# An attention and gated-MLP kernel: the order of its last six batches written out piece by piece

## The chip, the cores and the metric

The kernel runs on one core of one Trainium2 chip. The metric is the device time of one execution in microseconds (us). The core has TensorE for matrix products (PE in the rows, its weight loads PEld), VectorE (DVE), ScalarE (ACT), GpSimd (POOL) and SyncE (SP), which here only issues DMA transfers.

## The reference

Eight batches pass through three stages:

```python
# attention, 8 heads, 576 positions, 64 wide, 32 packed queries p
p_packed = sm_attn(p, k, v)               # softmax(p k^T / 8) v
out = sm_attn(q, p_packed, p_packed)      # softmax(q pp^T / 8) pp
x = out, heads side by side               # 576 x 512
# gated layer
gate = sigmoid(sum_k conv_w[k] * x shifted by 4 - k positions)
x = (gate * (x @ w_val)) @ w_out
# spatial MLP
h = relu(x @ w_in); u, v = halves of h    # 576 x 512 each
v_n = (v - mean(v)) / sqrt(var(v) + 1e-6)
v_s = w_spatial @ v_n + b_spatial         # mixes the 576 positions
return (u * v_s) @ w_out2
```

## The kernel before

All big products are made from pairs of a rounded value and its residue (`hi`, `lo`), three matmuls for each block of 128 rows: hi by hi, hi by lo, lo by hi (`mm3`, L120). The split into `hi` and `lo` is an ACT cast followed by a DVE subtraction (`split`, L114 and L116). The work of a batch is cut into pieces, each a Python generator; every `yield` ends one step of it. The pieces, in the order in which one batch needs them:

- `sa`: scores of the packed queries, 32 small matmuls into two PSUM tiles (64 records in the trace), then row maxima on DVE and the exponentials on ACT (L170 to L194). `tr`, `av`, `ppt`: transpose, product with v, transposed result `pp`.
- `sb`, `sn`, `sb2`: second attention, its softmax, and the matrices `A` in hi and lo.
- `m`: product of pp and w_val (`Mh`, `Ml`). `xt`: the attention's output x. `cv`: the convolution of x as four DVE operations in place on one tile `acc` (L350), then the gate (a sigmoid on ACT). There are four `cv`, one for each block of 128 channels.
- `val`: value products, 12 matmuls of 288 columns each, the product with the gate (L380), the split into g tiles, a copy of the tail.
- `hv`: 12 matmuls of 512 columns for each of four blocks of positions, 8 for the tail; normalization (statistics on DVE, a power on POOL, a DVE scaling, split) into `vn`. `hu`: 24 matmuls for each of four blocks, and a relu into `u`.
- `sp`: the spatial product, 28 matmuls for each of four blocks; then product with u (L480) and split into g tiles. `out`: the output product, 24 matmuls for each of four blocks; ACT copy, DMA out.

Pieces that belong to the attention of batch b+1 run beside the MLP of batch b, and next to the last pieces of batch b the `val` of batch b+1 begins. `lk`, `lq`, `lv`, `lp` issue loads on SP's queue for batches still further ahead. In the head there are also the conversion of the float64 weights (`uo`, `uw`, `uv`, `uu`: an ACT operation, three DVE operations, a POOL addition), products of two weight matrices (`fold`), and the setup of `ws` and `wo`.

Shared tiles set limits: four PSUM tiles serve all pieces, and four g tiles hold first the split values (`val`), then the split results of `sp`. A value of the next batch can therefore not be split before the last `out` matmul of this one has read its g tiles.

Two rules set the order. The string HEAD is taken literally, token by token (`tc.manual_schedule`): `0sp3.1` takes one step of piece sp3 of batch 0, `0sp3` the rest of it. The string LOOP is run for each batch from 2 to 7 outside of that, and there a scheduler reorders single instructions by a timeline of its own, so that matmuls of two pieces can alternate.

Of the kernel before, what the change touches and what calls it, by code (L numbers as in the profile page):

```python
# [20 lines left out]
HEAD = """
ro1.1 cb0.1 ip0 ro0 ic0 ik0 rw1 rw0.1 uo2.1 ik1 uo2.1 lk0 uo0.1 lp0 uo2 uo0.1 uo1.1 ro1 cw0.1 iv1 uo1.1 uo0 iv0 cw0.1
uw2.1 uo1 rv0.1 uw2.1 cw0 uw3.1 rv0 cb0.1 uw3.1 uw0.1 uw2 rw0 cb0.1 sa0.1 uw0.1 uw3 lq0 cb0.1 uw0 sa0.1 lq1 0ws2.1 cb0
uo3.1 0ws3.1 uo3.1 sa0.1 0ws0.1 sa0 tr0 uo3 0ru0.1 av0.1 tr1 uv0.1 0ru0 uv0.1 av1.1 uv1.1 lv0 av0.1 uv0 av1.1 av0.1
uw1.1 0ws4.1 av0 av1.1 ppt0.1 av1 uv1.1 lv1 ppt0 sb0 uw1.1 0lp0 uv1 0ru1.1 rv1.1 uw1 fv1.1 sn0.1 rv1 0uu0.1 fv1.1 lk1
sn1.1 sn0 0ws1.1 fv1.2 sb20.1 0wo0.1 sn1 fv0.1 fv1.1 0ru1 fv0.2 fv1 sb20.1 fv0.1 sb21.1 fv3.1 fv0.1 uv2.1 fv3.2 uv3.1
uv2.1 fv3.1 sb21.1 cx0.1 fv3.1 sb21 uv2 fv3 fv0 sb20 cx1.1 uv3.1 cx0 0uu0.1 uv3 m0.1 cx1 0uu0 fv2.1 0uu1.1 fv2.1 m0.1
0uu1.1 fv2.2 m0 0uu1 0val3.1 fv2 0uu2.1 0val3.1 0uu2.1 0val0.1 0val1.1 0val3.1 0uu2 0val2.1 0val3.1 0val0.1 0val3
0uu3.1 0val2.1 0val0.1 0val1.1 0val2.1 0val0.1 0sa0.1 0uu3.1 0val2.1 0lq0 0val1.1 0uu3 0fu0.1 1lp0 0sa0.1 0lq1 0val1.1
0fu0.1 0wo0.1 0fu0.2 0fu3.1 0fu0.1 0val1 0fu3.1 0sa0.1 0fu0 0fu3.1 0val0 0fu3.1 0val2 0hv0.1 0fu3.1 0tr0 0sa0 0fu3  # L30
0wo0.1 0hv1.1 0hv0.1 0tr1 0wo1.1 0wo0.1 0hv0.2 0fu2.1 0hv0.1 0hv1.1 0hv0.1 0fu2.1 0hv1.1 0wo1.1 0fu2.1 0wo1.1 0hv1.1
0fu2.1 0hv3.1 0hv1.1 0wo3.1 0fu2.1 0wo1.1 0hv0 0hv1.1 0wo1.1 0hv1 0fu2 0hv4.1 0hv3.1 0wo3.1 0hv3.1 0hv2.1 0wo3.1
0hv4.1 0hv3.1 0hv4.1 0lk0 0wo3.1 0hv3.1 0hv4.1 0av0.1 0wo3.1 0hv4.1 0av1.1 0hv3.1 0lv0 0fu1.1 0hv3 0lv1 0hv4.1 0av0.1
0hv2.1 0fu1.1 0hv4.1 0av0 0av1.1 0hv4.1 0fu1.1 0hv2.1 0av1 0ppt0.1 0fu1.1 0hv4 0ppt0 0hv2.2 0sb0 0ws3.1 0wo1 0fu1.1
0ws3 0m0.1 0ws4.2 0fu1 0lk1 0hv2.1 0wo2.1 0sn1.1 0hu0.1 0ws0.1 0ws2.1 0m0.1 0hu0.1 0ws4.1 0m0 0sn1 0ws4.1 0hu1.1 0hu0
0sb21.1 0ws4.1 0wo2.1 0hu1.1 0ws1.1 0wo0.1 0hu2.1 0hu1 0wo2.1 0sb21.1 0hu3.1 0ws2 1lq0 0wo2.1 0ws4 0hu3.1 0wo2.1 0ws1
0hu2.1 0sb21 0hu3 0wo3 0hv2 1sa0.1 0hu2 0ws0 0sn0.1 1lq1 0sp2.1 1lk1 0sp2.1 1sa0.1 0sn0 0sp0.1 1lk0 0sb20.1 1sa0.1
0sp0.1 1sa0 0sp3.1 0sp2.1 0sb20.1 0sp0.1 0sp2.1 0sb20 0sp1.1 0sp0.1 0sp2 0sp0 0sp1.1 1tr0 1tr1 0wo0 0xt0.1 0sp1.1
0sp3.1 0wo2 0sp1.1 0xt0 0sp1 0xt1.1 0sp3.1 1av0.1 0sp3.1 1av1.1 0xt1 1av0.1 1lv0 0sp3 0out2.1 1lv1 1av0 1av1.1 0cv1.1
0cv3.1 0cv1.1 0out2.1 1av1 0cv2.1 0cv0.1 0out3.1 0out2 0cv3.1 0cv1 0out0.2 0cv2.1 0cv3 0out1.1 0out0 0out1.1 0cv0.1  # L40
0cv2 1val1.1 0out1.1 1val1.1 0out1 0out3.1 1val1.1 0cv0 1val1.1 1val0.1 0out3.1 1val1 1val0.1 0out3 1val2.1 1val0.1
1val2.1 1val0.1 1ppt0.1 1val0 1val3.1 1ppt0 1val2.1 1val3.1 1val2.1 1sb0 1val3.1 1val2 1val3.1 1m0.1 1val3 1hv1.1
1sn0.1 1m0 1sn0 1hu1.1 1sn1.1 1hv0.1 1hv1.2 1sn1 1hv3.1 1sb21.1 1hv0.1 1hv1.2 1hv2.1 1sb21.1 1hv0.1 1hv1.1 1sb21
1hv0.1 1hv1 1hv0.1 1hu0.1 1hv3.1 1sb20.1 1hv0.1 1hu0.1 1hv0 1sb20.1 1hu1.1 1hv3.1 1hv2.1 1hu0 1hv2.1 1hv4.1 1hu1
1hv3.2 1hv2.1 1sb20 1hv3.1 1hu2.1 1hv3 1hv2.1 1hv4.1 1hv2.1 1hu3.1 1hv4.1 1hv2 1hv4.2 1hu3.1 1hv4.1 1hu2.1 1hu3 1hv4
1sp1.1 1hu2 1sp1.1 1sp2.1 1sp1 1sp2.1 1sp3.1 1sp2 1sp0.2 1xt0.1 1sp0.1 1sp3.1 1sp0.1 1xt0 1sp0 1xt1.1 1sp3.2 1xt1 1sp3
1out0.1 1cv1.1 1out0.1 1cv3.1 1cv1.1 1cv0.1 1out3.1 1out0.1 1cv2.1 1out0 1out3.1 1cv3.1 1cv1 1out2.1 1out3 1out1.1
1cv0.1 1cv3 1out1.1 1out2.1 1cv2.1 1cv0 1out1 1out2 1cv2
"""
# [712 lines left out]
```

## Time and profile before

| what | value |
|---|---|
| median of 3 runs (lowest, highest) | 615.42 us (615.08, 616.09) |
| profiled execution, its time | 615.56 us |
| span of that execution in the trace | 613.6 us |
| TensorE matmul busy | 581.7 us, 95% of the span |
| VectorE, ScalarE busy | 451.1 us (74%), 291.9 us (48%) |
| granted TensorE clock, all slices | full |

The time is taken outside of the trace and is about 2 us longer than the span. Busy time of TensorE is modelled from starts of matmuls, so a matmul that occupies it longer than it needs is counted as busy.

### The profile page before, as it was taken

What the parts mean: (1) busy time and instruction counts of PE and PEld (TensorE: products, weight loads), DVE (VectorE), ACT (ScalarE), POOL (GpSimd) and SP (SyncE); (2) the same over time, 40 slices, a digit from 0 to 9 for tenths busy, and PEclk for the clock granted to TensorE, in tenths of its full rate; (3) what the DMA queues carried; (4) which work ended last, traced back from release to release, by engine and by line L of the source; (5) the groups of instructions that cost most, each with busy time, mean ns of one, the idle gap of its engine ahead of it and who ended that gap; (6) DMA issues with size and microseconds to landing.
All of it is one profiled execution on the core that took longest, in us unless ns stands there. A gap on an engine that the chain in (4) does not pass through costs nothing.

```text
span 613.6 us, 12468 instructions
## 1 busy us (share of the span) xinstructions
PE 581.7 (95%) x5267; PEld 507.2 (83%) x5267; DVE 451.1 (74%) x868; ACT 291.9 (48%) x503; POOL 54.7 (9%) x72
## 2 busy tenths in 40 slices
...
GB/s 315 409 373 3 95 126 182 90 1 72 171 1 21 59 83 154 12 59 103 89 78 20 62 80 164 2 60 96 89 78 20 74 25 2 1 78 2 1 1 77
DMA packets 16615, 52.55 MB, mean 86 GB/s; under 512 B 1968, under 2 KB 2992, under 8 KB 16560
## 3 DMA queue, kind: packets, MB, share of 16 engines
...
q8 instruction: 41, 0.67, 0.4%
...
## 4 chain that ended last, share of the span: by engine, by line
PE 74%; DVE 7%; ACT 3%; issue 1%; ACTq 0%
PE ps L120 68%; DVE acc L350 2%; PE ps L170 2%; PE ps L311 1%; DVE mx L178 1%; PE ps L213 1%; ACT L194 1%; PE ps L248 1%; PE ps L295 1%; ACT a L194 1%; DVE g L116 1%; ACT g L114 1%; DVE nb L189 1%; DVE m L184 1%; DVE g L480 0%
## 5 line engine op out<-in xcount | busy, mean ns | idle before, releaser
L120 PE MATMUL ps<-ws,vn 128*128 128x288 f32 (+1 forms) x896 | 124.0, 296 | 0.0
L120 PEld LDWEIGHTS ps<-ws,vn 128*128 128x128 f32 (+1 forms) x896 | 120.2, 188 | 3.5 <-issue 3.4
L120 PE MATMUL ps<-g,wp 128*128 128x288 f32 x768 | 112.4, 297 | 0.8 <-DVE wp L568 0.8
L120 PEld LDWEIGHTS ps<-g,wp 128*128 128x128 f32 x768 | 106.5, 188 | 5.3 <-DVE wp L568 1.7
L120 PEld LDWEIGHTS ps<-g,wo 128*128 128x128 f32 x768 | 102.2, 188 | 5.5 <-issue 2.6
L120 PE MATMUL ps<-g,wo 128*128 128x288 f32 x768 | 105.5, 296 | 0.3 <-DVE g L116 0.2
L120 PE MATMUL ps<-wp,g 128*128 128x512 f32 x384 | 97.8, 402 | 3.1 <-ACT a L194 2.7
L350 DVE SCALAR_TENSOR_TENSOR acc<-x,cw,acc 128x572 f32<-128x572 f32 (+3 forms) x112 | 84.7, 815 | 20.5 <-ACT acc L346 19.7
L120 PEld LDWEIGHTS ps<-wp,g 128*128 128x128 f32 x384 | 70.0, 188 | 22.5 <-ACT a L194 4.5
L114 ACT CAST g<-g 128x576 fp32r<-128x576 f32 x64 | 43.2, 675 | 77.8 <-DVE g L480 59.5
L427 POOL TENSOR_TENSOR rstd<-rstd,mhalf 128x1 f32<-128x1 f32 (+1 forms) x40 | 23.4, 587 | 464.0 <-DVE rstd L425 464.0
L116 DVE TENSOR_TENSOR g<-g,g 128x576 fp32r<-128x576 f32 x64 | 48.3, 756 | 12.5 <-ACT g L114 11.9
L421 DVE BATCH_NORM_STATS2 st<-vr 128x6 f32<-128x512 f32 (+1 forms) x40 | 27.5, 689 | 26.3 <-ACT vr L409 23.7
L480 DVE TENSOR_TENSOR g<-ps,u 128x576 f32<-128x576 f32 x32 | 24.0, 754 | 23.3 <-PE ps L120 23.3
L114 ACT CAST vn<-vr 128x512 fp32r<-128x512 f32 (+1 forms) x40 | 24.7, 618 | 30.1 <-DVE vr L429 29.9
L120 PE MATMUL ps<-Ah,Ml 128*128 128x288 f32 x128 | 37.9, 296 | 0.7 <-DVE Ml L116 0.7
L120 PE MATMUL ps<-Ah,Mh 128*128 128x288 f32 x128 | 38.1, 298 | 0.0
L120 PE MATMUL ps<-Al,Mh 128*128 128x288 f32 x128 | 37.8, 295 | 0.0
L429 DVE TENSOR_SCALAR vr<-vr,mv,rstd 128x512 f32<-128x512 f32 (+1 forms) x40 | 22.4, 560 | 19.7 <-POOL rstd L427 19.7
L116 DVE TENSOR_TENSOR vn<-vr,vn 128x512 fp32r<-128x512 f32 (+1 forms) x40 | 28.2, 708 | 10.0 <-ACT vn L114 9.9
L409 ACT ACTIVATE vr<-ps 128x512 f32<-128x512 f32 x32 | 19.4, 607 | 31.3 <-PE ps L120 18.1
L505 ACT COPY o<-ps 128x576 f32<-128x576 f32 x32 | 20.2, 635 | 27.7 <-PE ps L120 27.7
...
## 6 DMA issues: line engine op xcount, KB each, us to landing
v<-vT SPq DMA_DIRECT2D x16, 650.0 KB, 5.7
...
```

The costliest lines, as they stand in the source:

```text
L114: nc.scalar.copy(out=hi, in_=src)
L116: nc.vector.tensor_tensor(out=lo, in0=src, in1=f32(hi), op=ALU.subtract)
L120: nc.tensor.matmul(out, lhsT=a, rhs=b, start=(i == 0), stop=(i == len(pairs) - 1))
L170: nc.tensor.matmul(ps[g][NPK * qt:NPK * qt + NPK, h // 2, SQ * (h % 2):SQ * (h % 2) + SQ], lhsT=pT_, rhs=k[:, SQ * qt:SQ * qt + SQ], start ...
L194: nc.scalar.activation(out=a[:, SQ * h:SQ * h + SQ], in_=ps[g][:, h // 2, SQ * (h % 2):SQ * (h % 2) + SQ], func=AF.Exp, scale=scale, bias= ...
L350: nc.vector.scalar_tensor_tensor(out=acc[:, sft:], in0=x[:, :S - sft], scalar=cw[:, c, tap:tap + 1], in1=acc[:, sft:], op0=ALU.mult, op1=A ...
L409: nc.scalar.activation(out=vr, in_=ps, func=AF.Relu)
L421: nc.vector.bn_stats(st[:w], vr[:w])
L427: nc.gpsimd.tensor_tensor(out=rstd[:w], in0=rstd[:w], in1=mhalf[:w], op=ALU.pow)
L429: nc.vector.tensor_scalar(out=vr[:w], in0=vr[:w], scalar1=mv[:w, 0:1], scalar2=rstd[:w], op0=ALU.subtract, op1=ALU.mult,)
L480: nc.vector.tensor_tensor(out=halves(t), in0=ps[:, :, :SH], in1=halves(self.u.pop(c)), op=ALU.mult)
L505: nc.scalar.copy(out=halves(t), in_=ps[:, :, :SH])
```

## The change

LOOP is gone. HEAD is replaced by another literal order for the setup and batches 0 to 3. A new string STEP is run three times with `first` = 3, 4, 5, and a new string LAST once with 6; digits in the tokens are added to `first`. All are taken literally, and a token without a number now means one step. No piece is changed: each issues the same instructions as before, in the same order within itself.

```diff
 HEAD = """
-ro1.1 cb0.1 ip0 ro0 ic0 ik0 rw1 rw0.1 uo2.1 ik1 uo2.1 lk0 uo0.1 lp0 uo2 uo0.1 uo1.1 ro1 cw0.1 iv1 uo1.1 uo0 iv0 cw0.1
...
+cb0 ro0.2 ik0.2 ip0.2 ro1 ik1.2 lk0.2 ro1 ic0.2 uo0 iv1.2 uo0 uo1 iv0.2 uo1 uo0 rw1 uo1 rw1 uo2 rv0 uo2 sa0 rv0 uo2
...
 """
-LOOP = """
-lq0 val1 val0 val2 lp0 val3 hu1 sa0 lq1 hv0 tr0 hv1 hu0 hv4 av0 tr1 av1 hu2 hv2 ppt0 hv3 sb0 sn0 sn1 sb20 sp1 lv0 sb21 hu3 sp0 sp3 sp2 m0 lk1 xt0 out1 lv1 xt1 cv0 cv1 cv2 cv3 out2 out0 lk0 out3
+STEP = """
+1val0.2 0out1 0out3 0out1 1val0 0out1 0cv1 0cv3 0out3 1val1 0out3 0out2 0out3 0cv2 0cv3 0out2 1val0 0out2 1val0 0cv2
...
+LAST = """
...
+1sp3 1sp2.3 1sp3.3 1out0.2 1out1 1out0.2 1out1 1out3 1out1.2 1out3 1out2 1out3.2 1out2.3
 """
...
+    live = {}
...
-    def run(order, batch):
-        live = {}
+    def run(order, first):
         for tok in order.split():
             tok, _, n = tok.partition(".")
-            name = tok.lstrip("01")
-            b = batch if len(name) == len(tok) else int(tok[0])
-            if tok not in live:
-                live[tok] = steps(b, name[:-1], int(name[-1]))
-            for _ in itertools.islice(live[tok], int(n) if n else None):
+            name = tok.lstrip("01234567")
+            b = -1 if len(name) == len(tok) else first + int(tok[0])
+            key = b, name
+            if key not in live:
+                live[key] = iter(steps(b, name[:-1], int(name[-1])))
+            for _ in itertools.islice(live[key], int(n or 1)):
                 pass
...
     with tc.manual_schedule():
-        run(HEAD, -1)
-    for b in range(2, B):
-        run(LOOP, b)
+        run(HEAD, 0)
+        for b in range(3, 6):
+            run(STEP, b)
+        run(LAST, 6)
```

The lines of the functions lie 22 further down in the changed file (L120 becomes L142).

First place: TensorE, the scores `sa` for the next batch (`kq`, `pbd`), which stand between the value products (`Ah`, `Mh`) and the first `hu` and `hv` products (`wp0`, `wp1` with `g`). Before, in the first turn of the loop:

```order
L120 MATMUL ps2_2396<-Ah_1857,Ml_1775 128x288
L120 MATMUL ps2_2415<-g_2371,wp0_101 128x288
L170 MATMUL ps2_2442<-kq_1301,pbd_718 32x144 x8
L170 MATMUL ps2_2442<-kq_1254,pbd_718 32x144 x5
L170 MATMUL ps2_2443<-kq_1301,pbd_718 32x144 x8
L170 MATMUL ps2_2443<-kq_1254,pbd_718 32x144
L120 MATMUL ps2_2415<-g_2371,wp0_101 128x288
L120 MATMUL ps2_2415<-g_2371,wp1_102 128x288
...
L170 MATMUL ps2_2443<-kq_1254,pbd_718 32x144 x4
```

In the change, in a STEP:

```order
L142 MATMUL ps2_4013<-Ah_3661,Ml_3815 128x288
L192 MATMUL ps2_4034<-kq_3586,pbd_2463 32x144
L192 MATMUL ps2_4035<-kq_3586,pbd_2463 32x144
...
L192 MATMUL ps2_4034<-kq_3279,pbd_2463 32x144
L192 MATMUL ps2_4035<-kq_3279,pbd_2463 32x144
...
L142 MATMUL ps2_4078<-wp0_101,g_3982 128x512
```

The scheduler had put matmuls of one PSUM tile (one half of the array's rows) behind each other and six `hu` matmuls among them; now the two tiles alternate sixteen times, as in the piece's own loops, and nothing stands between.

Second place: VectorE, the convolution `cv` of the next batch beside the `out` products. Before, in the last turn of the loop that has one:

```order
L116 TENSOR_TENSOR Ml_6221<-ps2_6211,Mh_6220 128x1024
L350 SCALAR_TENSOR_TENSOR acc_6278<-x_6234,cw_103,acc_6278 128x572
L350 SCALAR_TENSOR_TENSOR acc_6286<-x_6234,cw_103,acc_6286 128x572
L350 SCALAR_TENSOR_TENSOR acc_6278<-x_6234,cw_103,acc_6278 128x573
L350 SCALAR_TENSOR_TENSOR acc_6286<-x_6234,cw_103,acc_6286 128x573
L350 SCALAR_TENSOR_TENSOR acc_6294<-x_6235,cw_103,acc_6294 128x572
```

In the change, in a STEP:

```order
L138 TENSOR_TENSOR Ml_3815<-ps2_3787,Mh_3814 128x1024
L372 SCALAR_TENSOR_TENSOR acc_3846<-x_3798,cw_103,acc_3846 128x572
L372 SCALAR_TENSOR_TENSOR acc_3846<-x_3798,cw_103,acc_3846 128x573
L372 SCALAR_TENSOR_TENSOR acc_3846<-x_3798,cw_103,acc_3846 128x574
L372 SCALAR_TENSOR_TENSOR acc_3846<-x_3798,cw_103,acc_3846 128x575
L372 SCALAR_TENSOR_TENSOR acc_3848<-x_3798,cw_103,acc_3848 128x572
```

The four operations of one `acc` stood apart, with operations of another `acc` between them; now they follow each other directly, each on the result of the one before.

Third place: TensorE at the end of the last batch, where the last `sp` matmuls (`ws`, `vn`) give way to the `out` matmuls (`wo20`, `wo21` with `g`). Before (g_6768 and g_6707 come from the first two `sp`, g_6802 and g_6836 from the last two):

```order
L120 MATMUL ps2_6805<-ws1_1019,vn1_763 128x288
L120 MATMUL ps2_6839<-g_6768,wo20_862 128x288
...
L120 MATMUL ps2_6839<-g_6707,wo20_862 128x288 x2
...
L120 MATMUL ps2_6867<-g_6707,wo20_862 128x288 x2
L120 MATMUL ps2_6867<-g_6707,wo21_863 128x288
L120 MATMUL ps2_6895<-g_6768,wo20_862 128x288 x2
...
L120 MATMUL ps2_6839<-g_6836,wo20_862 128x288
```

In the change (g_6835 comes from the last `sp`):

```order
L142 MATMUL ps2_6676<-ws1_1012,vn1_763 128x288
L142 MATMUL ps2_6838<-g_6811,wo20_893 128x288 x2
L142 MATMUL ps2_6838<-g_6811,wo21_894 128x288
L142 MATMUL ps2_6838<-g_6746,wo20_893 128x288 x2
L142 MATMUL ps2_6838<-g_6746,wo21_894 128x288
L142 MATMUL ps2_6838<-g_6830,wo20_893 128x288 x2
L142 MATMUL ps2_6838<-g_6830,wo21_894 128x288
L142 MATMUL ps2_6838<-g_6835,wo20_893 128x288 x2
```

Before, the products with the first two g tiles were made for all four `out` tiles before any of them took a g tile of the last two `sp`; now the first `out` runs through all four g tiles at once, and the tenth of its matmuls reads the one that the `sp` just above has made.

## Rows read from the trace of the kernel before

**Rows 1.** The page: span, and busy time of each engine

```profile
span 613.6 us, 12468 instructions
PE 581.7 (95%) x5267; PEld 507.2 (83%) x5267; DVE 451.1 (74%) x868; ACT 291.9 (48%) x503; POOL 54.7 (9%) x72
```

**Rows 2.** Waits of PE: us in total, times, longest

```profile
PE ps L619 <- POOL cw L533: 13.9, 1, 13.9
...
PE ps L120 <- ACT a L194: 2.7, 5, 0.6
```

**Rows 3.** PE timeline, one loop batch: start, us, operation, [idle before <-releaser]

```profile
343.73 0.29 PE L120 MATMUL ps<-Ah,Mh 128*128 128x288 f32 x1
...
350.10 0.30 PE L120 MATMUL ps<-g,wp 128*128 128x288 f32 x1
350.33 1.45 PE L170 MATMUL ps<-kq,pbd 64*32 64x144 f32 x48
351.71 1.07 PE L120 MATMUL ps<-g,wp 128*128 128x288 f32 x6
352.71 0.69 PE L170 MATMUL ps<-kq,pbd 64*32 64x144 f32 x16
353.33 1.20 PE L120 MATMUL ps<-wp,g 128*128 128x512 f32 x4
...
359.20 3.06 PE L120 MATMUL ps<-wp,g 128*128 128x512 f32 x12 [0.55 <-ACT a L194]
362.10 3.36 PE L120 MATMUL ps<-g,wp 128*128 128x288 f32 x24
...
397.04 1.09 PE L295 MATMUL ps<-wval,ppT 64*32 64x512 f32 x16
...
402.10 0.74 PE L311 MATMUL ps<-an,pp 32*64 32x288 f32 x16
...
412.42 0.29 PE L120 MATMUL ps<-Ah,Mh 128*128 128x288 f32 x1
```

**Rows 4.** PE timeline, batches 0 and 1 under the literal order

```profile
109.38 1.24 PE L170 MATMUL ps<-kq,pbd 64*32 64x144 f32 x64
110.54 13.27 PE L120 MATMUL ps<-ws,vn 128*128 128x288 f32 x98
...
192.44 0.74 PE L311 MATMUL ps<-an,pp 32*64 32x288 f32 x16
```

**Rows 5.** DVE and ACT timelines: literal order (195.80), loop batch (398.52, 404.37)

```profile
195.80 12.37 DVE L350 SCALAR_TENSOR_TENSOR acc<-x,cw,acc 128x572 f32<-128x572 f32 x15 [1.00 <-ACT acc L346]
...
398.52 1.01 ACT L114 CAST Mh<-ps 128x1024 fp32r<-128x1024 f32 x1
...
404.37 10.99 DVE L350 SCALAR_TENSOR_TENSOR acc<-x,cw,acc 128x572 f32<-128x572 f32 x15 [3.58 <-ACT acc L346]
```

**Rows 6.** Timeline of all engines, end of the last batch

```profile
596.86 12.89 PE L120 MATMUL ps<-g,wo 128*128 128x288 f32 x96
597.06 0.76 DVE L480 TENSOR_TENSOR g<-ps,u 128x576 f32<-128x576 f32 x1 [0.28 <-PE ps L120]
597.85 0.68 ACT L114 CAST g<-g 128x576 fp32r<-128x576 f32 x1 [1.86 <-DVE g L480]
598.56 0.76 DVE L116 TENSOR_TENSOR g<-g,g 128x576 fp32r<-128x576 f32 x1 [0.74 <-ACT g L114]
...
609.78 0.64 ACT L505 COPY o<-ps 128x576 f32<-128x576 f32 x1 [1.62 <-PE ps L120]
```

**Rows 7.** DVE and PE timelines, the head

```profile
8.15 0.43 DVE L525 TENSOR_SCALAR tmp<-tmp 128x512 int32<-128x512 int32 x1 [1.42 <-ACT tmp L519]
...
32.79 0.83 DVE L261 STREAM_TRANSPOSE sT<-ps 128x288 f32<-128x288 f32 x2
...
56.15 0.40 PE L120 MATMUL ps<-Ah,Ml 128*128 128x288 f32 x1 [0.70 <-DVE Ml L116]
```

**Rows 8.** The page, DMA issues: count, KB, us from issue to landing

```profile
v<-vT SPq DMA_DIRECT2D x16, 650.0 KB, 5.7
```

More of the change, by code (lines that the diff above doesn't have):

```diff
@@ L21 @@
 HEAD = """
-ro1.1 cb0.1 ip0 ro0 ic0 ik0 rw1 rw0.1 uo2.1 ik1 uo2.1 lk0 uo0.1 lp0 uo2 uo0.1 uo1.1 ro1 cw0.1 iv1 uo1.1 uo0 iv0 cw0.1
[L23 to L46, printed above, removed]
@@ L47 @@
-1out0.1 1cv1.1 1out0.1 1cv3.1 1cv1.1 1cv0.1 1out3.1 1out0.1 1cv2.1 1out0 1out3.1 1cv3.1 1cv1 1out2.1 1out3 1out1.1
-1cv0.1 1cv3 1out1.1 1out2.1 1cv2.1 1cv0 1out1 1out2 1cv2
-"""
-LOOP = """
-lq0 val1 val0 val2 lp0 val3 hu1 sa0 lq1 hv0 tr0 hv1 hu0 hv4 av0 tr1 av1 hu2 hv2 ppt0 hv3 sb0 sn0 sn1 sb20 sp1 lv0 sb21 hu3 sp0 sp3 sp2 m0 lk1 xt0 out1 lv1 xt1 cv0 cv1 cv2 cv3 out2 out0 lk0 out3
+cb0 ro0.2 ik0.2 ip0.2 ro1 ik1.2 lk0.2 ro1 ic0.2 uo0 iv1.2 uo0 uo1 iv0.2 uo1 uo0 rw1 uo1 rw1 uo2 rv0 uo2 sa0 rv0 uo2
@@ new lines @@
+sa0 0ws4 uo3 rw0 cw0 rw0 cw0 0ws0 sa0 uo3 cw0 sa0 cb0 lq0.2 tr0.2 uo3 cb0 uw2 tr1.2 cb0 lq1.2 uw2 uw3 0ws1 uw3 uw2 uv0
+0ru0 uv0 uv1 uw3 lp0.2 av1 0lp0.2 cb0 uv1 uv0 uw0 av0 lv0.2 av1 uv1 av0 av1 uw1 av1 0ru1 av0 0ru1 ppt0 av0 uw0 ppt0
+lv1.2 uw1 uw0 sb0.2 0ru0 sn1 uw1 fv1 rv1 0uu0 fv3 rv1 lk1.2 fv1 0wo0 sn0 sn1 fv1 0ws2 fv1 fv3 0ws3 fv1 sb21 sn0 fv3.2
+fv2 fv3 fv1 sb21 fv2 fv3 fv0 sb21 sb20 uv2 fv2.2 uv3 fv0 fv2 cx1 uv2 sb20 uv3 uv2 0uu0 fv0 uv3 cx1 fv0 fv2 0uu0 sb20
+m0 0uu2 cx0 fv0 0uu2 m0.2 0uu2 fv0 cx0 0val2.2 0uu1 0val3 0val2 0val0 0uu1 0val2 0val3 0val2 0val0 0uu1 0val3 0val1
@@ new lines @@
+0val0 0val3 0sa0 0val0 0val3 0uu3 0lq0.2 0val1 0val0 1lp0.2 0lq1.2 0uu3 0val1 0uu3 0fu3.3 0sa0 0val1 0fu0 0wo0 0fu3
+0fu0 0fu3 0fu0 0fu3 0sa0 0fu0 0val1 0hv0 0wo0 0fu0 0tr0.2 0wo1 0sa0 0wo0 0fu0 0hv4 0tr1.2 0hv0.2 0hv1 0hv4 0hv0 0wo1
+0hv4 0hv0 0hv4 0wo1 0hv0 0av0 0hv4 0wo3 0wo1 0hv2 0lv0.2 0av0 0hv4 0hv0 0av0 0wo1 0hv4 0hv1 0hv4 0hv1 0fu2 0wo3 0hv4.2
+0fu2 0hv1 0wo3 0hv2 0fu2.2 0hv2 0lk0.2 0wo3 0hv3 0fu2 0hv1 0hv2 0wo3 0fu2 0hv1 0hv2 0hv1 0hv2 0av1 0hv2 0hv3 0fu1 0hv3
+0lv1.2 0fu1 0av1 0hv3 0av1 0fu1 0hv3.2 0ppt0 0fu1 0hv3 0ppt0 0m0 0ws4 0wo1 0fu1 0wo3 0ws4 0sb0.2 0ws0 0fu1 0ws3 0ws0
@@ new lines @@
+0hu0 0m0 0lk1.2 0sn1 0wo2 0wo0 0ws4 0hu0 0ws1 0m0 0sn1 0hu1 0hu0 0ws4.2 0sb21 0hu1 0ws2 0wo2 0hu2 0hu1 0ws2 0sb21
+0ws4.2 0hu3 0wo2 0hu3 0ws1 1lq0.2 0wo2 0sb21 0hu2 0hu3 0wo2 0ws3 0sp3 0hu2 0wo0 0sn0 0sp2 0wo2 0sn0 0sp2 0sb20 0sp1
+0sp2 0sb20 0sp1 0sp2 0sb20 0sp2 0sp0 0sp1.3 0sp0 0xt0 0sp0 0sp3 0sp0 0xt0.2 0sp0 0xt1 0sp3.2 0xt1.2 0sp3 0out3 0cv1
+0out2 0cv2 0cv1 0cv0 0out2 0cv3 0out0 0out2 0cv3 0cv1 0out2 1val1 0out0 0cv2 0cv3 1val3 0out0 1val1 0out0 1val3 0out3
+1val1 0cv2 1val3 0cv0 0out1 0out3.2 0out1 1val1 1val3 1val1 0out1 1val3 0cv0 1val0 1val2 0out1 1val0 1val2 1val0 1sa0
@@ new lines @@
+1val0 1val2 1val0 1val2 1lq1.2 1val2 1hv2 2lp0.2 1lk1.2 1sa0 1hu3 1hv2.2 1hv1 1sa0 1hv2.2 1sa0 1tr0.2 1hu1 1hv1 1tr1.2
+1hv2 1hv0 1hv1 1hv2 1hv1.3 1hu3 1hv0 1hv1 1hv0 1av1 1hu3 1hv0 1av0 1lv0.2 1av1 1hv3 1hv0 1av1 1lv1.2 1av0 1hv0 1av0
+1hv0 1hv4 1hv3.2 1hu0 1hv4 1hv3 1hv4 1hv3 1hv4 1ppt0 1hu2 1ppt0 1hv4 1hv3.2 1hv4 1hu0 1hv4.2 1hu1 1hv4.2 1hu0 1hu2
+1hu1 1sb0.2 1hu2 1m0 1sn1 1lk0.2 2lq0.2 1sp0 1m0 1sn0 1sn1 1sp3 1sp2 1m0 1sn0 1sb21 1sp3 1sp1 1sp3 1sb21 1sb20 1sp3
+1sp0 1sp1 1sp0 1sb20 1sp3 1sp0 1sb20 1xt0 1sp1 1sp2 1sp0 1sp1 1sb21 1xt0.2 1sp1 1xt1 1sp2.2 1xt1.2 1sp2 1cv0 1cv3 1cv0
@@ new lines @@
+1cv1 1cv2 1cv1 1cv0 2val0 1out0 1out1 1out0 1out3.2 1out0.2 1cv3 1cv1 1out2 1out3.2 1out1 1cv2 1cv3 2val0 1out1.2
+2val0 1cv2 2val2 2val1.2 1out2 2val1 2val0 2val1 2val0 2val2 1out2 2val1 2val3 1out2 2val2 2val3 2val2 2sa0 2val3
+2val2 2val3 2lq1.2 2val3 2hv0 3lp0.2 2lk1.2 2sa0 2hv2 2hv0.2 2sa0 2hv3 2hv0.2 2sa0 2tr0.2 2hv2 2tr1.2 2av0 2hv0 2hv2
+2av1 2lv0.2 2hu1 2av0 2lv1.2 2hv2 2hv0 2av0 2hv2 2hv3 2av1 2hv1 2hv2 2hv3 2av1 2hv2 2hv3.3 2hv4 2hv1 2hv3 2hv1 2hu2
+2hv4 2hv1 2hv4 2hv1 2hv4 2ppt0 2hu1 2hv1 2hv4 2ppt0 2hv1 2hv4 2sb0.2 2hu1 2hv4.2 2hu3 2sn1 2lk0.2 3lq0.2 2hu3 2hv4.2
```

22 lines of the change are left out of this document (added).

## The prediction

> **What bounds the kernel now.** I read the page first: the matmuls of TensorE fill 581.7 of 613.6 us [rows 1], so only 31.9 us are idle, and an order can win there or by making matmuls occupy the array for less time. Then I read the waits of PE, to see where the idle time lies. One wait at the start, for the converted convolution weights, is 13.9 us; in the loop there is a single repeated one, 2.7 us in five times, for the exponentials that free a PSUM tile [rows 2]. The copy and the DMA behind the last matmul take the last 3.85 us (613.6 less 596.86 + 12.89) [rows 1, 6]. What is left, 25.3 us, lies almost wholly in the head. Third, the timeline of PE, one batch long, for time that is busy but not needed. From the first `val` of one batch to that of the next is 412.42 - 343.73 = 68.69 us [rows 3]; the five batches 2 to 6 have such a period, and the last, without a next one beside it, runs from two periods later, 549.80, to 609.75.
>
> **What a loop batch gives back.** (a) `sa`. From its first matmul to the first `hv` behind it are 353.33 - 350.33 = 3.00 us, and the six `hu` matmuls inside would by themselves take 0.80, at 0.133 each (96 `out` matmuls in 12.89 [rows 6]); 2.20 us remain for 64 records [rows 3]. Under the literal order, with the two halves of the array alternating, the same 64 take 110.54 - 109.38 = 1.16 us [rows 4]. Saving 1.04; it is a measurement of the same piece in the same program, so I let it vary only from 0.9 to 1.1. (b) The wait of 0.55 us in `hv`. It comes because `sa` holds two of the four PSUM tiles until its exponentials are done, while `hu` and `hv` want the others. In the change four `hv` come first, two of them in the remaining tiles, the third in the tile that the first has left, the fourth in that of the first four exponentials. Twelve `hv` take 2.90 us [rows 3], so the fourth starts 8.7 us behind `sa`, and the exponentials were done before the wait's end at 359.20, 5.9 us behind it; 0.55 goes, bound 0 to 0.55. (c) The two `xt` were apart, with `out` between; now `xt`, `m`, `xt` stand together. One visit to the small-tile shape less: entering it costs 0.1 (0.23 from the single `hu` to `sa`, where 0.133 is usual [rows 3]), and I take as much for leaving: 0.2, bounds 0.1 to 0.3. (d) Alternation of single `hv` and `hu` matmuls. Between 353.33 and the start of the wait (359.20 - 0.55) stand 12 `hv` and 17 `hu`; at 2.90 us for twelve `hv` in a row (362.10 - 359.20) and 0.133 they need 5.16, and took 5.32 [rows 3]. 0.16, bounds 0 to 0.3. Together 1.95 us a batch, 9.75 for five.
>
> **What a STEP asks of the other engines.** I count from Z, the end of the last `sp` matmul. PE then has `xt`, `m`, `xt` (1.02 for `m`, 0.67 for each `xt`, 2.35 in all [rows 3]), 96 `out` and 48 `val` matmuls (19.15), and `sa` (1.25): the first `hv` can start at Z + 22.75. Its sixth matmul reads the residue of the second value tile, at Z + 24.0. Against it runs the convolution. Under the literal order the first tap came 195.80 - 192.44 = 3.36 us after the second `xt` began [rows 4, 5]; here that `xt` begins at Z + 1.6, and ACT has the cast of `Mh`, 1.01 us [rows 5], in front of the copies of x: first tap at Z + 5.0 to 6.0, I take 5.4, as part of the cast runs while the `xt` does. The sixteen taps now follow each other on their own results. 15 of them in that order took 12.37 us, 0.825 each; 15 interleaved in the loop took 10.99, 0.733 [rows 5]. So they end, with a product of 0.7 among them, at Z + 19.3. Gate 0.7, then product, product, residue, product, residue, 0.76 each and up to 0.1 overlapped (the forms of [rows 6]): Z + 23.7. Spare: 0.3 us. A similar count for the g tile of the last `sp` (two earlier `sp` and the copies of x queue in front of it) comes to Z + 3.4 for its residue, wanted at Z + 3.7. Both fit with little to spare; I charge 0.2 us a batch, 1.0 for five, bounds 0 and 1.2 a batch. The seven loads and four stores of a STEP are those of the loop, on the same SP queue, each load directly behind the piece that frees its buffer; the longest lands in 5.7 us [rows 8], and its user comes more than 10 us later, so they cost nothing; without that cover a batch would wait up to those 5.7.
>
> [...]
>
> **The last batch.** It loses what the scheduler did well. There is no `sa` in it, so the first `hv` follows `val` directly, 1.25 us earlier than in a STEP: 1.0 us of waiting for the same residue. And behind the last `sp` the `out` starts at once: the tenth and eleventh matmul, 1.2 and 1.33 us later, read the last g tile. DVE is by then still at the residue of the third `sp`, so that product (0.76), cast (0.68) and residue (0.76) [rows 6] end at about 0.8 + 2.2 = 3.0: waits of 1.0 and 0.65. Before, 24 matmuls of four `out` pieces, 3.2 us, covered this chain of 2.3, and there was no wait behind 596.86 [rows 6]. Cost 2.65, bounds 1.5 and 3.2.
>
> **The head.** DVE works from 8.15 us to the first transpose of the second softmax, 32.79, with no idle entry between the two rows, and the first value products wait for DVE at 56.15 [rows 7]. The same pieces stand in front of both in the new order (ten conversions, the small weights, first scores, transposes). The new order loads keys before the third weight block, so the scores come about 5 us earlier, but two conversions then wait for their loads; one such wait was 1.42 us [rows 7]. I see about 1.5 us more of DVE idle before the transpose, and the first `fold` and the `val` later by as much. Bounds: -2.5, if the earlier scores let PE use its idle 13.9 us, and +4.0, two more such waits. Nothing in the remaining pieces of batches 0 and 1 is charged: both versions have them in literal order.
>
> **Sum.** 615.56 - 9.75 + 1.0 + 2.65 + 1.5 = 610.96 us of the profiled kind; the median lies 0.14 below that execution, so 610.8, and I say 610.9.
>
> **Rivals.** *All fits.* No new wait in the five steps, 1.5 in the last batch, the head 1 us better: 615.42 - 9.75 + 1.5 - 1.0 = 606.2. For it: both handoffs of the step fit in my count; against it: the spare of 0.3 is smaller than what I can read off rows. 20%. *Paid back.* The head costs 4, the last batch 3.2 and the steps 0.5 each: 615.42 - 9.75 + 9.7 = 615.4. 10%. *VectorE becomes the bound (slower).* The convolution chain between the `xt` and the `hv` is the place; it is now one file of 16 taps, four gates and eight splits. Each us that it exceeds the cover of 24.0 is a us a batch. The gain is gone at (9.75 - 2.65 - 1.5) / 5 = 1.1 us a batch; at 1.6 the time is 617.8. For it: DVE's taps get longer in this order and ACT serves outputs, gates and casts in one queue; against it: DVE is idle for 3.58 us before the taps in the loop [rows 5], so there is room on it, and each part of the chain has its duration in a row. 13%. My forecast, from 607.5 to 614, has 52%; 5% is left for times beyond all these.
>
> A measurement of this kernel can tell about 0.2%, 1.2 us, from no change. Faster by more: 77% (the forecast, the first rival and most of what is left over); within: 10%; slower: 13%. The range 605.0 to 615.6 takes in the bounds of the single costs and leaves 2 in 10 outside; the forecast's own is 607.5 to 614.
>
> **What would show it.** In the profile after: all `sa` at about 1.2 us for 64 records; no wait for the exponentials in the steps; 66.9 us from `val` to `val`; in the last batch a wait of `hv` for a DVE residue near 1 us and of `out` near 1.6; `sa` as the first PE work, near 9 us, but the first `fold` near 33. The forecast is wrong if steps wait by more than 0.5 us for DVE (the chain), if the period stays above 68 without waits (then the small tiles were not the cost), or if the first value products start 3 us earlier or later than 56.

## The result, and the profile after

The changed kernel takes 609.52 us, the median of four executions (608.68 to 612.08); four of the kernel before beside them give 615.60 (615.08 to 616.09). The ratio is 0.9902 with a 95% interval of 0.9888 to 0.9917: faster by 1.0%, some 6 us. The profiled execution took 608.68, which is 6.88 less than the profiled one of before.

The page of the changed kernel, its span, the busy time of each engine and the granted clock of TensorE in 40 slices:

```profile
span 606.9 us, 12478 instructions
...
PE 575.4 (95%) x5267; PEld 505.1 (83%) x5267; DVE 466.9 (77%) x868; ACT 290.0 (48%) x503; POOL 58.3 (10%) x72
...
PEclk9999999999999999999999999999999999999999
```

TensorE is busy 6.3 us less than in [rows 1], with the same number of matmuls. So most of the gain is not idle time that was filled; it is time in which the array was occupied for longer than needed.

The waits of PE in the changed kernel (us in total, times, longest):

```profile
PE ps L192 <- DMA pbd<-pT: 7.9, 1, 7.9
PE ps L261 <- ACT pp L249: 6.1, 1, 6.1
PE ps L641 <- POOL cw L555: 4.3, 1, 4.3
PE ps L317 <- DVE wp L590: 2.1, 1, 2.1
PE ps L142 <- DVE g L138: 1.5, 3, 1.0
...
PE ps L142 <- ACT g L136: 0.8, 1, 0.8
...
```

The fivefold wait for the exponentials of [rows 2] is gone, and no other takes its place in the steps: all that is here belongs to the head, to batch 0 (0.16 us of the waits for g tiles) or to the last batch (the rest of those for g tiles). One batch on PE, against [rows 3]:

```profile
391.29 0.74 PE L333 MATMUL ps<-an,pp 32*64 32x288 f32 x16
391.96 1.09 PE L317 MATMUL ps<-wval,ppT 64*32 64x512 f32 x16
392.98 0.74 PE L333 MATMUL ps<-an,pp 32*64 32x288 f32 x16
393.65 5.03 PE L142 MATMUL ps<-g,wo 128*128 128x288 f32 x36
...
412.94 1.24 PE L192 MATMUL ps<-kq,pbd 64*32 64x144 f32 x64
414.11 11.47 PE L142 MATMUL ps<-wp,g 128*128 128x512 f32 x48
...
479.61 1.24 PE L192 MATMUL ps<-kq,pbd 64*32 64x144 f32 x64
```

The two `xt` stand around `m`, the scores occupy the array for 1.17 us in one piece, and 48 `hv` matmuls follow without a gap. From one `sa` to the next are 479.61 - 412.94 = 66.67 us, where [rows 3] gave 68.69. The same batch on DVE, from the end of the last `sp` (Z = 391.29, where the first `xt` starts), with the taps that answer to [rows 5]:

```profile
396.53 6.66 DVE L372 SCALAR_TENSOR_TENSOR acc<-x,cw,acc 128x572 f32<-128x572 f32 x8 [0.53 <-ACT acc L368]
403.10 0.75 DVE L402 TENSOR_TENSOR g<-ps,gate 128x576 f32<-128x576 f32 x1
403.77 6.65 DVE L372 SCALAR_TENSOR_TENSOR acc<-x,cw,acc 128x572 f32<-128x572 f32 x8
410.33 0.75 DVE L138 TENSOR_TENSOR g<-g,g 128x576 fp32r<-128x576 f32 x1
...
414.35 0.75 DVE L138 TENSOR_TENSOR g<-g,g 128x576 fp32r<-128x576 f32 x1
```

The first tap comes at Z + 5.24, the taps end at Z + 19.13, and the residue at 414.35, that of the second value tile (third in DVE's order), ends at Z + 23.81. The first `hv` starts at Z + 22.82, and its sixth matmul, which reads this residue, some 1.2 us later. The handoff fits, with about 0.2 us to spare.

The last batch, PE, with the waits that [rows 6] did not have:

```profile
546.20 1.32 PE L142 MATMUL ps<-wp,g 128*128 128x512 f32 x5
548.51 10.29 PE L142 MATMUL ps<-wp,g 128*128 128x512 f32 x43 [0.99 <-DVE g L138]
...
588.18 1.53 PE L142 MATMUL ps<-g,wo 128*128 128x288 f32 x9
590.54 0.40 PE L142 MATMUL ps<-g,wo 128*128 128x288 f32 x1 [0.84 <-ACT g L136]
591.33 11.68 PE L142 MATMUL ps<-g,wo 128*128 128x288 f32 x86 [0.40 <-DVE g L138]
```

Summed up by milestones, each the start of the last of the 48 value products of a batch. That of batch 2 starts at 212.46 us (212.60 before): the head and the first two batches give 0.14. From there to that of batch 7, five periods later, are 333.61 us, to 546.07, where before they were 343.42, to 556.02: they give 9.81, or 1.96 a batch (the first period is 66.87 us, the others 66.7). From there to the last ACT copy of the output are 56.98 us, 53.76 before: the last batch costs 3.22. Together 6.73; the rest of the 6.88 lies outside of these stretches.

### The profile page after: what moved, and what is told of

It is laid out like the page before. It is cut to its first block, busy times and chain, and to the rows that moved or that the text cites. A ratio compares the mean times of both kernels' runs of the same rounds, so it can differ in the third digit from the quotient of the medians.

```text
span 606.9 us, 12478 instructions
## 1 busy us (share of the span) xinstructions
PE 575.4 (95%) x5267; PEld 505.1 (83%) x5267; DVE 466.9 (77%) x868; ACT 290.0 (48%) x503; POOL 58.3 (10%) x72
## 3 DMA queue, kind: packets, MB, share of 16 engines
q1 hardware_dynamic: 16560, 51.77, 23.8%
## 4 chain that ended last, share of the span: by engine, by line
PE 73%; DVE 8%; ACT 2%; issue 1%; DVEq 0%
PE ps L142 68%; DVE acc L372 3%; PE ps L235 1%; DVE g L138 1%; PE ps L192 1%; PE ps L270 1%; PE ps L333 1%; DVE g L502 1%; ACT g L136 1%; PE ps L317 1%; ACT x L341 1%; DVE g L402 0%; DVE sT L283 0%; DVE sT L299 0%; DVE mx L285 0%
## 5 line engine op out<-in xcount | busy, mean ns | idle before, releaser
L142 PEld LDWEIGHTS ps<-ws,vn 128*128 128x128 f32 (+1 forms) x896 | 119.6, 188 | 3.6 <-ACT u L481 1.9
L142 PE MATMUL ps<-ws,vn 128*128 128x288 f32 (+1 forms) x896 | 122.3, 296 | 0.0
L142 PE MATMUL ps<-g,wo 128*128 128x288 f32 x768 | 107.1, 296 | 1.4 <-ACT g L136 0.8
L142 PE MATMUL ps<-g,wp 128*128 128x288 f32 x768 | 107.7, 297 | 0.3 <-DVE wp L590 0.3
L142 PEld LDWEIGHTS ps<-g,wo 128*128 128x128 f32 x768 | 103.1, 188 | 4.9 <-ACT x L341 2.2
L142 PEld LDWEIGHTS ps<-g,wp 128*128 128x128 f32 x768 | 104.3, 188 | 2.9 <-DVE wp L590 0.8
L372 DVE SCALAR_TENSOR_TENSOR acc<-x,cw,acc 128x572 f32<-128x572 f32 (+1 forms) x112 | 90.1, 816 | 7.6 <-ACT acc L368 4.6
L142 PE MATMUL ps<-wp,g 128*128 128x512 f32 x384 | 93.7, 400 | 1.0 <-DVE g L138 1.0
L142 PEld LDWEIGHTS ps<-wp,g 128*128 128x128 f32 x384 | 70.9, 188 | 20.5 <-DVE g L138 1.9
L449 POOL TENSOR_TENSOR rstd<-rstd,mhalf 128x1 f32<-128x1 f32 (+1 forms) x40 | 27.2, 681 | 441.5 <-DVE rstd L447 434.5
L142 PE MATMUL ps<-Ah,Mh 128*128 128x288 f32 x128 | 38.1, 298 | 0.6 <-DVE Ml L138 0.5
L142 PE MATMUL ps<-Ah,Ml 128*128 128x288 f32 x128 | 37.8, 295 | 0.0
L142 PE MATMUL ps<-Al,Mh 128*128 128x288 f32 x128 | 37.8, 295 | 0.0
L378 ACT ACTIVATE gate<-acc 128x576 f32<-128x576 f32 x28 | 19.2, 687 | 25.5 <-DVE acc L372 25.4
```

Source lines behind the costliest of these rows:

```text
L142: nc.tensor.matmul(out, lhsT=a, rhs=b, start=(i == 0), stop=(i == len(pairs) - 1))
L372: nc.vector.scalar_tensor_tensor(out=acc[:, sft:], in0=x[:, :S - sft], scalar=cw[:, c, tap:tap + 1], in1=acc[:, sft:], op0=ALU.mult, op1=A ...
L378: nc.scalar.activation(out=gt, in_=acc, func=AF.Sigmoid)
L449: nc.gpsimd.tensor_tensor(out=rstd[:w], in0=rstd[:w], in1=mhalf[:w], op=ALU.pow)
```

## Experiments

All but one change the order alone; that one adds products which nobody reads. The head differs from one execution to the next (last section), so each trace is also read in a stretch of its own: from the start of the scores of batch 3, behind the last value product of batch 2, to the start of the last matmul. In the changed kernel these are 390.03 us (212.69 to 602.72). This stretch repeats well: two experiments that touch the head alone gave 390.03 and 390.05, and one kernel profiled twice gave 387.03 and 387.04. A ratio is to the kernel before, run on the same chip as the experiment; a distance from the changed kernel is the difference of two ratios, times 615.6 us. For the grouped scores, the cut scores and the taps in turns the interval overlaps that of the changed kernel, so these three are read from the stretch of one profiled execution each.

**Scores, one half of the array after the other.** In `sa`, for batches 3 to 7:

```diff
+            pairs = [heads[i:i + 2] for i in range(0, 8, 2)]
+            if self.b > 2:
+                pairs = [[x] for g in range(2) for x in heads[g::2]]
-            for i in range(0, 8, 2):
+            for pair in pairs:
```

> The 16 score matmuls of one row half run behind each other, then the 16 of the other half, in the score pieces of batches 3 to 7; nothing else is moved. First theory (the lack of alternation between the two halves of the array was what the scores cost in the loop): the 64 records take 1.9 to 2.2 us in place of 1.17, each of the five batches about 0.8 to 1.0 longer, the time 4 to 5 us above the changed kernel's 609.5, near 614. Rival (the hu matmuls that split the scores in two were the cost, one more visit to the small shape): the records stay at 1.2 to 1.3 and the time within 1.5 us of 609.5.

The ratio is 0.9932 (0.9915 to 0.9950), 1.8 us above the changed kernel; the stretch grew by 2.13, with 0.48 more in each later period (67.15). The score rows, on PE and on its weight loads:

```profile
346.86 1.72 PE L195 MATMUL ps<-kq,pbd 64*32 64x144 f32 x64
```

```profile
346.86 1.43 PEld L195 LDWEIGHTS ps<-kq,pbd 64*32 64x32 f32 x64 [0.17 <-ACT g L136]
```

and the weight loads of the same 64 in the changed kernel:

```profile
412.94 0.94 PEld L192 LDWEIGHTS ps<-kq,pbd 64*32 64x32 f32 x64 [0.16 <-ACT g L136]
```

The scores now need 348.51 - 346.86 = 1.65 us instead of 1.17, and the 0.48 is just the growth of the weight loads, 0.49. Neither theory had the size: grouping is a real cost, and it is half of what (a) was to give back. The two rows show where alternating pays, in the weight loads (0.94 us with the halves alternating, 1.43 without); why the same 64 loads take longer in groups, no run shows.

**Scores cut in two.** In the three steps, one yield in `sa` behind 48 records, and in `hv0` one behind its first three matmuls:

```diff
+                if i == 3 * len(pairs) // 4 and self.b > 4:
+                    yield
...
+                    mm3(ps, blocks([0]), stop=False)
+                    yield
+                    mm3(ps, blocks(range(1, NC)), start=False)
...
-... 1val1 1sa0 1val3 1val1 ...
+... 1val1 1sa0 1hv0 1sa0 1val3 1val1 ...
```

> In the three steps the alternating scores are cut after 48 of the 64 records by three hv matmuls; nothing else moves. First theory (a second visit to the small shape costs 0.1 us on entering and 0.1 on leaving, and that is what the grouped scores, 1.66 us without a cut, lack of the 2.2 of before): the cut costs 0.2 us in each of three batches, 0.6 in all, time near 610. Rival (a cut costs more, 0.5 us each time, since the array empties twice): 1.5 us or more, near 611.

> Both at once in the three steps: the scores of one row half behind each other, and the same cut by three hv matmuls. If the two costs add up to what was read for the loop of before, the scores with their cut take 0.9 to 1.1 us more than now in each of three batches, 2.7 to 3.3 in all, time near 612.5. If they only add as measured for each by itself, with 0.5 for the grouping and 0.2 for the cut: 0.7 a batch, 2.1 in all, near 611.6.

The cut alone: ratio 0.9911 (0.9891 to 0.9931), stretch longer by 1.06, 0.35 for each of three batches, between the two expectations. Grouped and cut: ratio 0.9944 (0.9923 to 0.9966), stretch longer by 2.48, 0.83 for each of the three. The second kernel's rows:

```profile
345.98 1.24 PE L200 MATMUL ps<-kq,pbd 64*32 64x144 f32 x48
347.14 0.98 PE L143 MATMUL ps<-wp,g 128*128 128x512 f32 x3
348.05 0.69 PE L200 MATMUL ps<-kq,pbd 64*32 64x144 f32 x16
348.67 1.66 PE L143 MATMUL ps<-wp,g 128*128 128x512 f32 x6
```

The two parts of the scores take 1.16 and 0.62 us here, where [rows 3] has 1.38 and 0.62, and the three `hv` between them 0.91 where 0.73 is usual. The costs add up (0.48 + 0.35 = 0.83, between the two expectations), so of the 1.04 that (a) was to give, 0.8 are shown: 0.5 for weights of one row half behind each other, 0.35 for a second visit to the small shape. The remaining 0.2 stays open; it lies in the first 48 records, whose order in the loop was not this one.

**The second `xt` behind the first `out`.** In STEP and at the end of HEAD:

```diff
-... 1xt0.2 1xt1 1sp3 1m0 1sp3 1out0 1xt1.2 1m0 1out0 1cv0 ...
+... 1xt0.2 1sp3 1m0 1sp3 1out0 1m0 1out0 1xt1.3 1cv0 ...
```

> In the steps and at the end of the head the second xt comes behind the first out, 24 out matmuls (3.2 us) later than now, as it stood in the loop before. First theory (the convolution chain from the xt to the residue of the second value tile fits its cover with 0.2 to 0.3 us to spare): two of the four convolution tiles start some 3 us later, hv waits 2 to 3 us in each batch that has such an order, four in all, and the time rises by 8 to 13 us, to 618 to 622. Rival (the chain has room, since two tiles of the convolution can run before the second xt is needed): only the second visit to the small shape is paid, 0.2 us a batch, and the time stays within 1.5 us of 609.5.

Ratio 1.0092 (1.0075 to 1.0109), 11.7 us above the changed kernel and slower than before; the stretch grew by 13.82. Its waits in a step:

```profile
346.68 0.43 PE L192 MATMUL ps<-kq,pbd 64*32 64x144 f32 x2
348.12 1.22 PE L192 MATMUL ps<-kq,pbd 64*32 64x144 f32 x62 [1.01 <-DVE g L402]
349.26 1.42 PE L142 MATMUL ps<-wp,g 128*128 128x512 f32 x5
351.21 0.96 PE L142 MATMUL ps<-wp,g 128*128 128x512 f32 x3 [0.52 <-DVE g L138]
```

and its taps:

```profile
332.58 6.66 DVE L372 SCALAR_TENSOR_TENSOR acc<-x,cw,acc 128x572 f32<-128x572 f32 x8 [3.39 <-ACT acc L368]
```

The taps start 2.9 us later, and everything behind them moves by that much: the period is 417.51 - 348.12 = 69.39, longer by 2.7. The first theory holds, with part of the wait in a place that it did not name (the scores wait for a PSUM tile that a late value product holds). This is the slower rival of the forecast made to happen: the gain of a batch, 2.0 us, hangs on the place of one `xt`. Not all of the 13.82 is the chain, though. In the last batch `hv` waits 1.79 and 0.98 us, and behind the first of them the granted clock falls to 0.50, where it is from 559 to 565 us:

```profile
559.42 13.03 PE L142 MATMUL ps<-wp,g 128*128 128x512 f32 x43 [0.98 <-DVE g L138]
```

The same 43 take 10.29 us at the full clock in the changed kernel, so 2.7 us are the clock's and some 11.1 the chain's.

**Value products behind the output products.** In STEP and LAST:

```diff
-1val0.2 0out1 0out3 0out1 1val0 0out1 0cv1 0cv3 0out3 1val1 0out3 0out2 ...
+0out1 0out3 0out1 0out1 0cv1 0cv3 0out3 0out3 0out2 0out3 0cv2 0cv3 0out2.2 1val0.2 0cv2 1val0 ...
```

> The value products are no longer woven between the output products: in the steps and the last part all output products of a batch come first, then the value products of the next. First theory (weaving frees nothing that TensorE waits for, the gain came from the scores and small matmuls): the time stays within 1 us of 609.5. Rival (weaving is what gave the gain, by covering the split of the value products): 1.6 to 2 us a batch are lost, 8 us or more, near 618.

Ratio 0.9954 (0.9940 to 0.9968), 3.2 us above the changed kernel; the stretch grew by 2.96. DVE and PE in a step:

```profile
398.70 13.22 DVE L372 SCALAR_TENSOR_TENSOR acc<-x,cw,acc 128x572 f32<-128x572 f32 x16 [0.53 <-ACT acc L368]
411.84 0.75 DVE L402 TENSOR_TENSOR g<-ps,gate 128x576 f32<-128x576 f32 x1
...
417.37 0.75 DVE L138 TENSOR_TENSOR g<-g,g 128x576 fp32r<-128x576 f32 x1
```

```profile
348.89 1.43 PE L142 MATMUL ps<-wp,g 128*128 128x512 f32 x5
350.78 1.43 PE L142 MATMUL ps<-wp,g 128*128 128x512 f32 x5 [0.46 <-DVE g L138]
```

Both theories miss. The first value product now waits until all taps are done, so its split is no longer under them, and the residue of the second value tile ends at Z + 24.7 (417.37 + 0.75 less 393.47) in place of 23.8. The `hv` waits 0.46 us in each step, and the period is 0.7 longer (418.17 - 350.78 = 67.39). So weaving is worth 0.7 us a batch in this order: it is what makes the handoff fit, by a hair. It is not where the gain over before comes from.

**Taps in turns.** For batches from 4 on, a yield behind each tap, and `cv` tokens of two tiles in turns (here those of the first two tiles; the other two are treated alike at the start of STEP and LAST):

```diff
-... 1cv0 1cv1 1cv0 1out1 1cv2 1out0 1cv3 1out0 1cv1 1cv0
+... 1cv0 1cv1 1out1 1cv2 1out0 1cv3 1out0 1cv0 1cv1 1cv0 1cv1 1cv0 1cv1 1cv0 1cv1 1cv0
```

> In the batches from 4 on the four operations of one convolution tile alternate with those of another, so that none reads the result of the one just before it; the same operations in all. First theory (an operation that reads the result of the one before it starts later): such taps come 0.73 us apart in place of 0.82, the chain before the last batch's value split ends 1.2 to 1.5 us sooner, the last batch's hv wait of 1 us goes, the steps keep their period of 66.7; the time falls by 1.0 to 1.5 us, to about 608.3. [...]

Ratio 0.9877 (0.9854 to 0.9899), 1.5 us below the changed kernel; but the stretch shrank by 0.55 only, and the rest is within what the head differs by. The taps:

```profile
396.40 8.81 DVE L373 SCALAR_TENSOR_TENSOR acc<-x,cw,acc 128x572 f32<-128x572 f32 x12 [0.53 <-ACT acc L369]
...
405.79 3.00 DVE L373 SCALAR_TENSOR_TENSOR acc<-x,cw,acc 128x574 f32<-128x574 f32 x4
```

Twelve take 8.81, 0.734 each; in the changed kernel eight take 6.66, 0.83. The order of taps matters, by 0.1 us each. By itself a tap takes 0.82 us (the mean of the page): in turns the next one starts 0.09 us before the one ahead ends (11 steps of 0.73), and where it reads that one's result it starts 0.03 us behind its end (steps of 0.85). The taps end 1.5 us earlier by Z, as the first theory had it, but the last batch's `hv` wait fell only from 0.99 to 0.44, and the steps kept 66.7. The next link is in ACT's queue, whose rows behind the taps are

```profile
408.15 0.69 ACT L380 ACTIVATE gate<-acc 128x576 f32<-128x576 f32 x1 [2.55 <-DVE acc L373]
408.74 0.66 ACT L137 CAST g<-g 128x576 fp32r<-128x576 f32 x1
409.31 0.64 ACT L529 COPY o<-ps 128x576 f32<-128x576 f32 x1
409.84 0.69 ACT L380 ACTIVATE gate<-acc 128x576 f32<-128x576 f32 x1
```

Two tiles in turns end together, so their gates come together too, and the second one stands behind a cast and an output copy. DVE's product behind it starts at 410.59, only 0.55 earlier by Z than in the changed kernel (411.26).

**The last part reordered.** `hv` yields behind its first three matmuls, `out` behind those with three g tiles:

```diff
-... 1hv0 1hv1 1hv0.3 ...
+... 1hv0 1hv1 1hv2 1hv0 1hv1 1hv0.3 ...
...
-... 1out0.2 1out1 1out0.2 1out1 1out3 ...
+... 1out0.2 1out1.2 1out0.2 1out1 1out0.2 1out1 1out3 ...
```

> Last batch only: the first three hv make their products with the first g tile (three matmuls each) before any takes the second g tile, and the first two out make those with three g tiles before any takes the fourth. First theory (the last batch loses 3.3 us to two late g tiles and the refill of the array behind each wait): waits at both places vanish, and the time falls by 2.6 to 3.2 us, to about 606.5. Rival (the waits only move, since the chain behind them sets the end in any order): it falls by less than 1.5 us.

> The reordered last part (three hv and two out that take the early g tiles first) together with the convolution operations taken in turns between two tiles. The last part's waits are gone by the first change alone; the shorter convolution chain then only leaves more room. First theory: the time of the reordered last part alone, 606.0 to 606.7, within 0.5 us. Rival (the two add, another 0.7 to 1.4 us): 605.3 or below.

The first: 606.69 us, ratio 0.9846 (0.9829 to 0.9863); the stretch shrank by 3.00. Its PE rows at the two places:

```profile
547.10 6.23 PE L142 MATMUL ps<-wp,g 128*128 128x512 f32 x26
...
587.83 13.07 PE L142 MATMUL ps<-g,wo 128*128 128x288 f32 x96
```

No wait is left at either, as the first theory had it. From the last value product, 547.10, the matmuls of the last batch take 53.80 us (to 587.83 + 13.07), where before they took 53.59 (to 609.75). With the taps in turns as well: 606.76, ratio 0.9852 (0.9828 to 0.9875), stretch shorter by 2.96. The first theory holds here too: once nothing waits for the convolution, a shorter one is worth nothing.

**Load order in the head.** `ro` loads the first output weight in quarters, `ik` and `lk` keys:

```diff
-cb0 ro0.2 ik0.2 ip0.2 ro1 ik1.2 lk0.2 ro1 ic0.2 ...
+cb0 ro0.2 ro1.2 ik0.2 ip0.2 ik1.2 lk0.2 ic0.2 ...
```

and, in the second kernel, `cb0 ro0.2 ik0.2 ip0.2 ik1.2 lk0.2 ro1.2 ic0.2 ...`.

> Head only: the third and fourth quarter of the first output weight are loaded ahead of the keys. First theory (the head is bound by VectorE's file of conversions, which has its loads in time either way): the first transpose of the second softmax stays within 0.5 us of 32.84, with the scores 2 to 3 us later than 7.93. Rival (the scores' place sets the head): that transpose comes 2 us later or more.

> Head only: the third and fourth quarter of the first output weight are loaded behind all keys. The forecast charged 1.5 us for conversions that wait for their loads. First theory (the charge was right in kind, and was not paid only because the third quarter lands at 9.04, just in time for its conversion at 9.76): the third conversion now waits 2.5 to 3.5 us for its load, and the first transpose of the second softmax comes 2 to 3 us later, near 35. Rival (VectorE's file has slack that takes it up): it comes within 0.5 us of 32.84.

One execution each, read from its rows alone. Weights first: the scores start at 10.63 and the first transpose of the second softmax at 33.76, 0.9 later than in the changed kernel; neither expectation. DVE then waits 1.35 us for the scores. Weights last, the conversion that waits:

```profile
12.85 0.43 DVE L547 TENSOR_SCALAR tmp<-tmp 128x512 int32<-128x512 int32 x1 [3.66 <-ACT tmp L541]
```

The wait is 3.66, slightly more than the first theory had, and the transpose comes at 34.75, 1.9 later, slightly less. That is near the 1.5 of the forecast, whose charge was right in kind and is not paid by the changed order.

**Idle products in the head.** On top of the reordered last part, seven matmuls into a tile that nobody reads, before `ppt`:

```diff
+    def idle_products(_):
+        ps = ps2.tile([P, 2, 512], F32, tag="ps2", name="pd")[:, 0, :]
+        for _ in range(7):
+            nc.tensor.matmul(ps, lhsT=woT[0][:, :P], rhs=woT[1], start=True, stop=True)
+        yield
...
-... 0ru1 ppt0 av0 uw0 ppt0 ...
+... 0ru1 dm0 ppt0 av0 uw0 ppt0 ...
```

> The kernel with the reordered last part, and seven products that nobody reads put into TensorE's idle time ahead of the head's first transposed product (22.4 to 28.5 us). First theory (the first fold products run at half rate, 0.85 us each instead of 0.43, for one to more than six products after that idle time, differently in each execution): all fold products but the first run at 0.43, the first value products come at 55.9 to 56.0 in place of up to 58.9, and the time is 0.5 to 2 us below that of the reordered last part alone, with a smaller spread. Rival (the half rate comes from the small products just ahead of the folds): no change.

> The kernel with the reordered last part once more, beside the one with the seven idle products on the same chip: 606 to 607, by either theory.

With them 606.98 us, ratio 0.9853 (0.9831 to 0.9874); without them, on the same chip, 606.40, ratio 0.9840 (0.9822 to 0.9858). The rate came out as expected and the time did not. The fold products run at full rate from their start at 32.06 us, but VectorE's folded weights still end the wait ahead of `m`, and in this execution the granted clock is 0.57 from 52 to 56 us (0.50 from 53 to 55), where the 16 `m` matmuls take 1.66 us instead of 1.09:

```profile
32.06 1.98 PE L596 MATMUL ps<-winv,woT 128*128 128x512 f32 x4 [0.66 <-POOL winv L566]
...
51.67 1.66 PE L319 MATMUL ps<-wval,ppT 64*32 64x512 f32 x16 [2.06 <-DVE wp L601]
```

All four executions with the idle products list a mean granted clock of 0.997, of the four without them two do.

## Why the forecast held, point by point

The forecast was 610.9 (its own range 607.5 to 614), the median 609.5: the forecast's case, not a rival's. A distance of 1.4 us is less than the 3.4 us by which the four executions differ, so the median alone tests no term. Against the profiled execution, 608.68, the sum of 610.96 is 2.3 us too high, and its terms show where.

- **(a) to (d), 1.95 a batch, 9.75 in five.** Measured 9.81 in five, 1.96 a batch. Of (a) grouping and cut are shown by experiment, with 0.8 of 1.04; that `sa` takes 1.17 us in one piece, as [rows 4] said, is in the trace. (b): the wait for the exponentials is absent from the steps; it was not tried by itself. (c) can be read by comparing the two traces, from the first matmul of `m` or `xt` to the last value product, between which both have the same matmuls in two orders. The last one before, and in the change:

```profile
418.65 0.30 PE L120 MATMUL ps<-Ah,Ml 128*128 128x288 f32 x1
```

```profile
412.71 0.29 PE L142 MATMUL ps<-Ah,Ml 128*128 128x288 f32 x1
```

These are 418.65 - 397.04 = 21.61 us ([rows 3]) and 412.71 - 391.29 = 21.42, so 0.19 where 0.2 was forecast. (d) was only argued: 1.96 less 0.83, 0.55 and 0.19 leaves 0.39 for it (forecast 0.16) and the open 0.2 of (a).
- **The steps' wait, 0.2 a batch.** Not paid. Here the count itself was the best part of the forecast: first tap Z + 5.4 (5.24), end of taps 19.3 (19.13), residue 23.7 (23.81), spare 0.3 (0.2); and for the last `sp` a residue at 3.4 (394.62 less Z, 3.33). Since it fit, the term should have been zero by its own arithmetic; the 1.0 was a guess for the error of reading. The late `xt` and the value products behind show that the count was no accident: 2.9 us and 0.8 us more on the chain came out as 2.7 and 0.7 a batch.
- **The order of taps.** The forecast had both figures from rows of before ([rows 5]), and both came back: eight taps behind each other took 6.66, 0.83 each, and the taps in turns 0.734, the next one starting 0.09 us before the one ahead ends. Why a tap can start that early no run shows. The steps' wait vanished with the taps as slow as forecast, not by their order.
- **The last batch, 2.65.** The mechanism and the places were right and the size was off: 3.22, at the bound of 3.2. Idle time came to 0.99 in the `hv` and 0.84 + 0.40 in the `out`, 2.23 in all, less than the 2.65 forecast. But each stop costs more than its idle time: the nine `out` ahead of the first wait and the one behind it take 591.33 - 588.18 = 3.15 us, and ten take 1.33; 1.82 is lost where 1.24 is idle. Likewise five `hv` take 2.31 (548.51 - 546.20) where 1.21 is usual, 1.10 lost for 0.99. That is 2.92 of the 3.22; with both places reordered the stretch gave back 3.00.
- **The head, +1.5.** This step failed: it cost nothing (first transpose at 32.84, before 32.79). The two waits for loads that the forecast saw were 0.34 and 0.18 us, since the third quarter of the weight landed at 9.04 us, just ahead of its conversion; a third, for ACT, was 0.19. The wait of 1.42 us that the kernel before had [rows 7] went away, which the forecast did not set against its charge: from its first conversion to that transpose DVE is idle for 0.71 us, where it was for 1.42. Putting the quarter behind the keys brings the forecast's wait back. In the other direction the earlier scores did not help either: the first value products still wait for VectorE, at 55.88 ([rows 7]: 56.15).

So the sum was 1.6 too high up to the last value product of batch 2 (1.5 charged to the head, 0.14 gained) and 1.1 too high in the loop (1.0 charged for waits that did not come, 0.06 more gained), 0.6 too low in the last batch, and 0.15 lies outside of these stretches: 2.3 in all. That the last batch cancels a part of the others is luck.
